# Dense layer with squared ReLU: the first block's loads, transposes and tail columns arranged anew, w2 in three loads

## The chip, the cores and the metric

The kernel runs on one core of one Trainium2 chip. A core has five engines that run beside each other and meet at semaphores: TensorE (PE in the profile, with PEld for its weight loads), VectorE (DVE), ScalarE (ACT), GpSimd (POOL) and SyncE (SP), which here only issues transfers. Transfers run on 16 DMA engines. The metric is device time in microseconds (us), lower is better: the median over several executions.

## The reference

```python
# x (1, 2048, 576), w1 (576, 4608), b1 (4608), w2 (4608, 576), b2 (576), all bf16
h = jnp.einsum("bsd,df->bsf", x, w1) + b1
r = jnp.where(h > 0, h, 0)
h = r * r
out = jnp.einsum("bsf,fd->bsd", h, w2) + b2
```

Both products have 2048 x 576 x 4608 multiplications. The inner dimension of the first, 576, is four and a half times the 128 rows of TensorE's array.

## The kernel before

The 2048 rows of x are worked in four blocks of 512 (`SB`). For each block the kernel needs x transposed (`xTw`, 576 rows as nine slots of 64 on two halves of the partitions), computes the hidden values as 36 tiles of 128 columns of w1 (`hT`), and then multiplies by w2. Blocks 0 and 1 go first, hidden values of both and then the second product of both; blocks 2 and 3 follow in the same way.

Of the 36 hidden tiles, four (`G`) use full matmuls on `w1n`: 512 rows of w1 in four parts of 128 (index k), and the 64 rows left over in `w1n8`, used by two half-height matmuls side by side (`pair`, lines 203 and 205). The other 32 tiles are in `w1_h`: 16 columns j for the lower half of the partitions and 16 for the upper, and `a_rows` (line 179) runs for each j nine pairs of 64-row matmuls, lower and upper at once (lines 188 and 190). For this, most of x transposed has to stand on both halves of the partitions; `dup_windows` (lines 119 and 120) copies it over with VectorE. Each hidden tile is then read out by ScalarE (relu with the bias, line 176) and squared by VectorE (line 177).

Block 0 has its own start, since nothing is loaded yet; blocks 1 to 3 get x transposed by the DMA engines (`load_xT`). For block 0 the four x tiles of 128 rows are loaded as they are (`load_x`, line 72) and TensorE transposes them (`x_transpose`, line 149: four full 128-column parts each and, for the 64 tail columns, a fifth transpose of the last 128 columns), while ScalarE and VectorE copy the results out of PSUM (`x_copies`, lines 156 to 159). The first hidden tiles of block 0 are computed with k outermost and in two halves of 256 rows (`part(h, k)`, line 227: half h of the block, part k, four matmuls). The order on TensorE is written out by hand: seven warming matmuls on constants (line 63), transposes of tiles 0 and 1, part(0,0), transposes of tile 2, parts (0,1) and (0,2), transposes of tile 3, parts (0,3) and (1,0), the transpose of b1 (`make_b1T`, line 166), the remaining parts, the pairs, and then `a_rows(0)`.

All transfers keep their order in the program on the queue that issues them. SP's queue issues x tile 0, w1n parts 0 and 1, x tile 3, w1n parts 2 and 3; then w1_h columns j=0 for each half, w1n8 in two loads (line 79), w1_h to j=11, the transposed x of block 1, w1_h to j=15, b2 (line 304), w2 in six loads (line 134), and the transposed x of block 2. ScalarE's queue issues x tiles 1 and 2 ahead of its table load; GpSimd's issues b1's rows and a column of b2. An SP issue of w1_h is 144 or 288 KB, in runs of 256 or 512 bytes.

PSUM has eight banks, four in the pool `ps_h` and four in `ps_o`; a tile waits until an earlier one of its pool is read out.

Of the kernel before, what the change touches and what calls it, by code (L numbers as in the profile page):

```python
# [11 lines left out]
BF16 = mybir.dt.bfloat16  # L12
FP32 = mybir.dt.float32
# [4 lines left out]
def kernel(  # L18
# [9 lines left out]
    nc = tc.nc  # L28
    keep = tc.keep_in_program_order
    P = 128  # L30
    H = 64
    x2 = x.flatten_outer_dims()
    out2 = out.flatten_outer_dims()
    S, D = x2.shape
    F = w1.shape[1]
    NFT = F // P
    NC = D // H
    NK = NC // 2
    G = 4
    GW = G * P  # L40
# [4 lines left out]
    RT = SB // P  # L45
    DT = P
    DM = D - DT

    const = ctx.enter_context(tc.tile_pool(name="const", bufs=1))
    wpool = ctx.enter_context(tc.tile_pool(name="wpool", bufs=1))  # L50
# [5 lines left out]
    ps_h = ctx.enter_context(tc.tile_pool(name="ps_h", bufs=4, space=PSUM))  # L56
    ps_o = ctx.enter_context(tc.tile_pool(name="ps_o", bufs=4, space=PSUM))

    wps = ps_o.tile([P, 512], FP32, name="wps", tag="po")
    ones = nc.const_aps.tensor(1.0, [P, 512], BF16)  # L60
    WARM = [512] * 6 + [128]
    for i, n in enumerate(WARM):
        keep(nc.tensor.matmul(wps[:, 0:n], lhsT=ones[:, 0:P], rhs=ones[:, 0:n], start=True, stop=True))  # L63

    xs = const.tile([P, RT, D], BF16, name="x_sb")
    w1n = wpool.tile([P, NK, GW], BF16, name="w1n")
    w1n8 = wpool.tile([P, G // 2, P], BF16, name="w1n8")
    w1_h = wpool.tile([P, NC, FH], BF16, name="w1_h")
    w1_v = w1.rearrange("(c p) f -> p c f", p=H)

    def load_x(eng, rt):
        keep(eng.dma_start(out=xs[:, rt, :], in_=x2[rt * P:(rt + 1) * P, :]))

    def load_w1n(eng, k):
        keep(eng.dma_start(out=w1n[:, k, :], in_=w1[k * P:(k + 1) * P, 0:GW]))

    def load_w1n8(eng, h):
        src = w1[NK * P:D, 0:GW].rearrange("p (i h f) -> p i h f", h=2, f=P)
        keep(eng.dma_start(out=w1n8[h * H:(h + 1) * H, :, :], in_=src[:, :, h, :]))

    def load_w1(eng, h, j0, j1):
        keep(eng.dma_start(out=w1_h[h * H:(h + 1) * H, :, j0 * P:j1 * P],
                      in_=w1_v[:, :, GW + h * FH + j0 * P:GW + h * FH + j1 * P]))

    load_x(nc.sync, 0)
    load_x(nc.scalar, 1)
    load_w1n(nc.sync, 0)
    load_x(nc.scalar, 2)
    load_w1n(nc.sync, 1)
    load_x(nc.sync, 3)  # L90
    for k in range(2, NK):
        load_w1n(nc.sync, k)

    ident = const.tile([P, P], BF16, name="ident")
    make_identity(nc, ident[:])
    b1_rows = const.tile([P, P], BF16, name="b1_rows")
    nc.gpsimd.memset(b1_rows[:], 0.0)
    nc.gpsimd.dma_start(out=b1_rows[0:NFT, :], in_=b1.rearrange("(ft p) -> ft p", p=P))
    b2_col = const.tile([P, 1], BF16, name="b2_col")
    nc.gpsimd.dma_start(out=b2_col[:], in_=b2[DM:D].rearrange("(d o) -> d o", o=1))  # L100
    b2T = const.tile([P, 1], FP32, name="b2T")
    nc.gpsimd.tensor_copy(out=b2T[:], in_=b2_col[:])
    warm = const.tile([P, 1], FP32, name="warm")
    keep(nc.scalar.activation(out=warm[:], in_=nc.const_aps.tensor(0.0, [P, 1], FP32), func=ACT.Relu))

    E3, O, SPC, E = 0, 1, 5, 6
    LO_W = [O, O + 1, O + 2, O + 3, E, E + 1, E + 2, E3, SPC]
# [9 lines left out]
    def dup_windows(sb):  # L117
        xT = xT_blk[sb]
        keep(nc.vector.tensor_copy(out=xT[0:H, SPC:SPC + 4, :], in_=xT[H:P, E3:E3 + 4, :]))  # L119
        keep(nc.vector.tensor_copy(out=xT[H:P, SPC:SPC + 4, :], in_=xT[0:H, O:O + 4, :]))  # L120
# [7 lines left out]

    w2_sb = wpool.tile([P, NFT, D], BF16, name="w2_sb")
    w2_view = w2.rearrange("(ft p) d -> p ft d", p=P)  # L130
    W2CH = 6

    def load_w2(c):
        keep(nc.sync.dma_start(out=w2_sb[:, c * W2CH:(c + 1) * W2CH, :], in_=w2_view[:, c * W2CH:(c + 1) * W2CH, :]))
# [3 lines left out]
    alloc_xT(0)  # L138
    xT0 = xT_blk[0]
    HS = SB // 2  # L140
    tb_po = [ps_o.tile([P, 2, HS], BF16, name="tb", tag="po") for _ in range(2)]
    tb_ph = [ps_h.tile([P, 2, HS], BF16, name="tb", tag="ph") for _ in range(4)]
    half_banks = [tb_ph, None]

    def x_transpose(j, k):
        h, q = divmod(j, 2)
        qc = slice(q * P, (q + 1) * P)
        bank, slot, c0 = (half_banks[h][k], 0, k * P) if k < NK else (half_banks[h][2], 1, D - P)
        keep(nc.tensor.transpose(bank[:, slot, qc], xs[:, j, c0:c0 + P], ident[:]))  # L149

    def x_copies(h):
        hc = slice(h * HS, (h + 1) * HS)
        for k in range(NK):
            src = half_banks[h][k][:, 0, :]
            if k % 2 == 0:
                keep(nc.vector.tensor_copy(out=xT0[:, O + k, hc], in_=src))  # L156
            else:
                keep(nc.scalar.copy(out=xT0[:, O + k, hc], in_=src))
        keep(nc.vector.tensor_copy(out=xT0[:, E3, hc], in_=half_banks[h][2][:, 1, :]))


    b1T = const.tile([P, NFT], FP32, name="b1T")

    def make_b1T():
        b1T_ps = ps_o.tile([P, P], BF16, name="b1T_ps", tag="po")
        keep(nc.tensor.transpose(b1T_ps[:], b1_rows[:], ident[:]))  # L166
        keep(nc.vector.tensor_copy(out=b1T[:], in_=b1T_ps[:, 0:NFT]))

# [26 lines left out]
    def a_full(sb, order):  # L195
        xT = xT_blk[sb]
        banks = []
        for g in range(G):
            pool, tag = (ps_o, "po") if g < 2 else (ps_h, "ph")
            banks.append(pool.tile([P, SB], FP32, name="pn", tag=tag))  # L200

        def pair(i, start, stop):
            keep(nc.tensor.matmul(banks[2 * i][:], lhsT=w1n8[0:H, i, :], rhs=xT[0:H, SPC, :],  # L203
                             start=start, stop=stop, skip_group_check=order == "k_outer"))
            keep(nc.tensor.matmul(banks[2 * i + 1][:], lhsT=w1n8[H:P, i, :], rhs=xT[H:P, E3, :],  # L205
                             start=start, stop=stop, skip_group_check=order == "k_outer"))

        def full(g, k, start, stop):
            keep(nc.tensor.matmul(banks[g][:], lhsT=w1n[:, k, g * P:(g + 1) * P], rhs=xT[:, O + k, :],  # L209
                             start=start, stop=stop))  # L210

        if order == "rows_first":
            for i in (1, 0):
                pair(i, True, False)
            for g in (2, 3, 0, 1):
                for k in range(NK):
                    full(g, k, False, k == NK - 1)
                evac_h(sb, banks[g], g)
        else:
            if order == "k_outer":  # L220
                tb_new = [ps_h.tile([P, 2, HS], BF16, name="tb", tag="ph") for _ in range(2)]
                half_banks[1] = tb_new + tb_po

                def part(h, k):
                    hc = slice(h * HS, (h + 1) * HS)
                    for g in range(G):
                        keep(nc.tensor.matmul(banks[g][:, hc], lhsT=w1n[:, k, g * P:(g + 1) * P],  # L227
                                              rhs=xT[:, O + k, hc], start=(h == 0 and k == 0), stop=False,
                                              skip_group_check=True))

                for j in range(2):
                    for k in range(NK):
                        x_transpose(j, k)
                for j in range(2):
                    x_transpose(j, NK)
                x_copies(0)
                part(0, 0)
                for k in range(NK + 1):
                    x_transpose(2, k)
                part(0, 1)  # L240
                part(0, 2)
                for k in range(NK + 1):
                    x_transpose(3, k)
                x_copies(1)
                dup_windows(0)
                part(0, 3)
                part(1, 0)
                make_b1T()
                for k in range(1, NK):
                    part(1, k)  # L250
            else:
                for g in (2, 3, 0, 1):
                    for k in range(NK):
                        full(g, k, k == 0, False)
            for i in (1, 0):
                pair(i, False, True)
                evac_h(sb, banks[2 * i], 2 * i)
                evac_h(sb, banks[2 * i + 1], 2 * i + 1)
# [35 lines left out]
    for (j0, j1) in [(0, 1), (1, 2), (2, 4), (4, 6), (6, 8), (8, 10), (10, 12)]:  # L294
        load_w1(nc.sync, 0, j0, j1)
        load_w1(nc.sync, 1, j0, j1)
        if j0 == 0:
            load_w1n8(nc.sync, 0)
            load_w1n8(nc.sync, 1)
    load_xT(1)  # L300
    for (j0, j1) in [(12, 14), (14, 16)]:
        load_w1(nc.sync, 0, j0, j1)
        load_w1(nc.sync, 1, j0, j1)
    keep(nc.sync.dma_start(out=b2_bc[:], in_=b2.partition_broadcast(P)))
    for c in (0, 3, 1, 4, 2, 5):
        load_w2(c)
    load_xT(2)

# [51 lines left out]
```

## Time and profile before

| | |
|---|---|
| median of 7 executions | 291.11 us (290.91 to 291.48) |
| the profiled execution's own time | 291.04 us |
| its span, first to last instruction | 289.2 us |
| TensorE busy | 285.3 us, 2032 matmuls |
| TensorE weight loads busy | 159.0 us |
| ScalarE busy | 96.7 us |
| VectorE busy | 78.5 us |
| GpSimd busy | 2.3 us |
| DMA | 31637 packets, 16.52 MB |

Busy times are of one execution. A matmul's busy time overlaps that of the next, so TensorE's busy share says that it has work, not that it runs at its peak. In a line of groups, "xN" is the count, then come busy us, mean ns of one, and the engine's idle time just ahead of those instructions, with what ended most of it. In the chain of waits each line is a start, a length and what ran. "DMA to landing" is the time from a transfer's issue to the signal that all of it has arrived.

### The profile page before, as it was taken

To read this page: it belongs to the slowest core of one execution; us is meant where nothing else is said; L and a number is where in the kernel's file an instruction comes from. 1 tells how busy PE (TensorE), PEld (TensorE's weight loads), DVE (VectorE), ACT (ScalarE), POOL (GpSimd) and SP (SyncE) were. 2 spreads that over 40 slices of the span, in tenths; PEclk is the share of its full clock that TensorE was granted. 3 is DMA by queue.
4 is the path that set the end of the run, shared out by engine and by line. 5 is a ranking of instruction groups with operands and counts; after the bars stand their busy time and mean duration, and the time that the engine had idled before them with its cause. 6 is when DMAs were issued, how large, how long until landed. Compare 5 with 4: busy or idle time off the path is not lost.

```text
span 289.2 us, 4699 instructions
## 1 busy us (share of the span) xinstructions
PE 285.3 (99%) x2032; PEld 159.0 (55%) x2032; DVE 78.5 (27%) x176; ACT 96.7 (33%) x154; POOL 2.3 (1%) x10
## 2 busy tenths in 40 slices
PE   8999999999999999999999999999999999999995
PEld 5568888887444555555544444444444455555554
DVE  1644544444500200000025444444440001000001
ACT  3666666666400000000027666666670000000000
POOL 3000000000000000000000000000000000000000
PEclk9999999999999999999999999999999999999999
DMA  6999999700001100000000000000000110000000
GB/s 195 220 240 179 275 387 255 104 0 2 0 18 37 35 16 18 16 16 18 16 16 2 1 2 0 2 0 2 0 2 0 36 39 16 16 17 32 19 16 18
DMA packets 31637, 16.52 MB, mean 57 GB/s; under 512 B 15732, under 2 KB 31616, under 8 KB 31616
## 3 DMA queue, kind: packets, MB, share of 16 engines
q1 hardware_dynamic: 31264, 15.91, 22.6%
q8 instruction: 16, 0.26, 0.4%
q10 hardware_dynamic: 288, 0.30, 0.3%
q14 instruction: 5, 0.04, 0.0%
q0 software_dynamic: 64, 0.01, 0.0%
HBM read 11.36 MB, written 2.36 MB: 47 GB/s over the span
## 4 chain that ended last, share of the span: by engine, by line
PE 99%; DVE 0%; issue 0%
PE po L289 38%; PE ph L188 35%; PE pt L270 11%; PE ph L190 8%; PE pn L209 4%; PE pn L227 1%; PE wps L63 1%; PE pn L203 1%; PE tb L149 0%; DVE xTw L156 0%; DVE o_sb L291 0%; PE pn L205 0%; PE b1T_ps L166 0%
## 5 line engine op out<-in xcount | busy, mean ns | idle before, releaser
L190 PE MATMUL ph<-xTw,w_h 64*128 64x512 bf16 x576 | 124.7, 376 | 0.0
L188 PE MATMUL ph<-xTw,w_h 64*128 64x512 bf16 x576 | 124.6, 376 | 0.0
L289 PE MATMUL po<-w_sb,hT 128*128 128x448 bf16 (+2 forms) x612 | 109.4, 341 | 0.0
L176 ACT ACTIVATE r<-ph,b1T 128x512 bf16<-128x512 f32 x128 | 81.1, 685 | 41.6 <-PE ph L190 22.7
L289 PEld LDWEIGHTS <-hT 128*128 128x128 bf16 x612 | 58.5, 98 | 51.0
L177 DVE TENSOR_TENSOR hT<-r 128x512 bf16<-128x512 bf16 x144 | 61.2, 425 | 76.0 <-ACT r L176 75.8
L188 PEld LDWEIGHTS <-w_h 64*128 64x128 bf16 x576 | 54.1, 94 | 48.3
L190 PEld LDWEIGHTS <-w_h 64*128 64x128 bf16 x576 | 54.1, 94 | 0.2 <-DMA w_h<-in_w_dram 0.2
L291 DVE TENSOR_TENSOR o_sb<-po,b_bc 128x448 bf16<-128x448 f32 (+2 forms) x17 | 10.1, 597 | 125.8 <-PE po L289 125.8
L270 PE MATMUL pt<-hT,w_sb 128*128 128x512 bf16 x144 | 31.4, 379 | 0.0
L176 ACT ACTIVATE r<-pn,b1T 128x512 bf16<-128x512 f32 x16 | 10.3, 688 | 61.1 <-PE pn L205 59.6
L270 PEld LDWEIGHTS <-w_sb 128*128 128x128 bf16 x144 | 14.1, 98 | 17.0
L273 ACT ACTIVATE oT<-pt,b2T 128x512 bf16<-128x512 f32 x4 | 2.8, 688 | 28.3 <-PE pt L270 28.3
L209 PE MATMUL pn<-xTw,w1n 128*128 128x512 bf16 x48 | 10.9, 379 | 0.0
L209 PEld LDWEIGHTS <-w1n 128*128 128x128 bf16 x48 | 4.5, 97 | 6.0 <-issue 0.8
L227 PE MATMUL pn<-xTw,w1n 128*128 128x256 bf16 x32 | 4.2, 273 | 0.1
L63 PE MATMUL wps<-const-bfloat16-1.0 128*128 128x512 bf16 (+1 forms) x7 | 2.8, 581 | 0.8 <-PEq L344 0.8
L227 PEld LDWEIGHTS <-w1n 128*128 128x128 bf16 x32 | 2.9, 97 | 0.8 <-DMA w1n<-in_w_dram 0.3
L119 DVE COPY xTw<-xTw 64x2048 bf16<-64x2048 bf16 x4 | 2.8, 689 | 0.2
L120 DVE COPY xTw<-xTw 64x2048 bf16<-64x2048 bf16 x4 | 2.8, 688 | 0.1
L156 DVE COPY xTw<-tb 128x256 bf16<-128x256 bf16 x4 | 1.1, 292 | 5.9 <-PE tb L149 5.9
L203 PE MATMUL pn<-xTw,w1n 64*128 64x512 bf16 x8 | 2.4, 379 | 0.0
(23 smaller groups left out, 14.3 us busy)
## 6 DMA issues: line engine op xcount, KB each, us to landing
w_sb<-in_w_dram SPq DMA_DIRECT2D x6, 864.0 KB, 11.2
w_h<-in_w_dram SPq DMA_DIRECT2D x14, 288.0 KB, 5.7
out_dram<-o_sb SPq DMA_DIRECT2D x15, 112.0 KB, 1.7
w_h<-in_w_dram SPq DMA_DIRECT2D x4, 144.0 KB, 3.5
w1n<-in_w_dram SPq DMA_DIRECT2D x4, 128.0 KB, 3.3
out_dram<-ot SPq DMA_DIRECT2D x4, 128.0 KB, 2.0
x_sb<-in_x_dram ACTq DMA_DIRECT2D x2, 144.0 KB, 3.1
x_sb<-in_x_dram SPq DMA_DIRECT2D x2, 144.0 KB, 3.1
```

The source lines that it names most:

```text
L63: keep(nc.tensor.matmul(wps[:, 0:n], lhsT=ones[:, 0:P], rhs=ones[:, 0:n], start=True, stop=True))
L119: keep(nc.vector.tensor_copy(out=xT[0:H, SPC:SPC + 4, :], in_=xT[H:P, E3:E3 + 4, :]))
L176: keep(nc.scalar.activation(out=r[:], in_=bank[:], func=ACT.Relu, bias=b1T[:, ft:ft + 1], scale=1.0))
L177: keep(nc.vector.tensor_tensor(out=hTs[sb][:, ft, :], in0=r[:], in1=r[:], op=ALU.mult))
L188: keep(nc.tensor.matmul(bx[:], lhsT=w1_h[0:H, LO_C[i], jc], rhs=xT[0:H, LO_W[i], :], start=(i == 0), stop=(i == NC - 1)))
L190: keep(nc.tensor.matmul(by[:], lhsT=w1_h[H:P, UP_C[i], jc], rhs=xT[H:P, UP_W[i], :], start=(i == 0), stop=(i == NC - 1)))
L203: keep(nc.tensor.matmul(banks[2 * i][:], lhsT=w1n8[0:H, i, :], rhs=xT[0:H, SPC, :], start=start, stop=stop, skip_group_check=order == "k_o ...
L209: keep(nc.tensor.matmul(banks[g][:], lhsT=w1n[:, k, g * P:(g + 1) * P], rhs=xT[:, O + k, :], start=start, stop=stop))
L227: keep(nc.tensor.matmul(banks[g][:, hc], lhsT=w1n[:, k, g * P:(g + 1) * P], rhs=xT[:, O + k, hc], start=(h == 0 and k == 0), stop=False, s ...
L270: keep(nc.tensor.matmul(pt[:], lhsT=w2_sb[:, ft, DM:D], rhs=hT[:, ft, :], start=(i == 0), stop=(i == NFT - 1)))
L289: keep(nc.tensor.matmul(po[:, 0:d1 - d0], lhsT=hT[:, ft, jj * P:(jj + 1) * P], rhs=w2_sb[:, ft, d0:d1], start=(i == 0), stop=(i == NFT - 1)))
L291: keep(nc.vector.tensor_tensor(out=o_sb[:, d0:d1], in0=po[:, 0:d1 - d0], in1=b2_bc[:, d0:d1], op=ALU.add))
```

## The change

The diff changes block 0's start and two loads further on:

- Loads. x tile 0 comes in two pieces of columns, 0 to 255 on SP's queue and 256 to 575 on ScalarE's. All four x tiles are issued ahead of w1n (tiles 1 and 3 on SP, tile 2 on ScalarE). w1n comes in three loads, k=0 and k=2,3 on ScalarE's queue, k=1 on SP's. w1n8 comes in one load on SP's queue ahead of all of w1_h; it now holds all 512 columns on both halves of the partitions, and its source reads the 64 rows of w1 twice. b1's rows are loaded from ScalarE's queue after its table load, b2's column from SP's after w1_h.
- Transposes. All four x tiles are transposed, four parts each, ahead of the first part(0,0). Copies out of PSUM are VectorE's, but for the last two, ScalarE's. The tail columns of two x tiles are first put side by side by GpSimd (`xs8`), so that one transpose does both; four VectorE copies put them into place.
- Duplicates. `dup_windows(0)` is replaced by one ScalarE copy of three slots (`dup_windows_first`), one VectorE copy of four and one of one.
- One warming matmul fewer; PSUM tiles of the start move from `ps_o` to `ps_h`, and block 0's four first banks are all in `ps_o`.
- w2 comes in three loads of twelve row tiles.

The diff, cut to its core:

```diff
...
     ps_h = ctx.enter_context(tc.tile_pool(name="ps_h", bufs=4, space=PSUM))
     ps_o = ctx.enter_context(tc.tile_pool(name="ps_o", bufs=4, space=PSUM))
-    wps = ps_o.tile([P, 512], FP32, name="wps", tag="po")
+    wps = ps_h.tile([P, 512], FP32, name="wps", tag="ph")
     ones = nc.const_aps.tensor(1.0, [P, 512], BF16)
-    WARM = [512] * 6 + [128]
+    WARM = [512] * 5 + [128]
     for i, n in enumerate(WARM):
         keep(nc.tensor.matmul(wps[:, 0:n], lhsT=ones[:, 0:P], rhs=ones[:, 0:n], start=True, stop=True))
     xs = const.tile([P, RT, D], BF16, name="x_sb")
     w1n = wpool.tile([P, NK, GW], BF16, name="w1n")
-    w1n8 = wpool.tile([P, G // 2, P], BF16, name="w1n8")
+    w1n8 = wpool.tile([P, GW], BF16, name="w1n8")
     w1_h = wpool.tile([P, NC, FH], BF16, name="w1_h")
     w1_v = w1.rearrange("(c p) f -> p c f", p=H)
-    def load_x(eng, rt):
-        keep(eng.dma_start(out=xs[:, rt, :], in_=x2[rt * P:(rt + 1) * P, :]))
-
-    def load_w1n(eng, k):
-        keep(eng.dma_start(out=w1n[:, k, :], in_=w1[k * P:(k + 1) * P, 0:GW]))
-
-    def load_w1n8(eng, h):
-        src = w1[NK * P:D, 0:GW].rearrange("p (i h f) -> p i h f", h=2, f=P)
-        keep(eng.dma_start(out=w1n8[h * H:(h + 1) * H, :, :], in_=src[:, :, h, :]))
+    def load_x(eng, rt, c0=0, c1=D):
+        keep(eng.dma_start(out=xs[:, rt, c0:c1], in_=x2[rt * P:(rt + 1) * P, c0:c1]))
+
+    def load_w1n(eng, k0, k1):
+        src = w1[k0 * P:k1 * P, 0:GW].rearrange("(k p) f -> p k f", p=P)
+        keep(eng.dma_start(out=w1n[:, k0:k1, :], in_=src))
+
+    def load_w1n8(eng):
+        src = w1[NK * P:D, 0:GW].unsqueeze(0).broadcast_to([2, H, GW])
+        keep(eng.dma_start(out=w1n8[:, :], in_=src))
     def load_w1(eng, h, j0, j1):
         keep(eng.dma_start(out=w1_h[h * H:(h + 1) * H, :, j0 * P:j1 * P],
                       in_=w1_v[:, :, GW + h * FH + j0 * P:GW + h * FH + j1 * P]))
-    load_x(nc.sync, 0)
-    load_x(nc.scalar, 1)
-    load_w1n(nc.sync, 0)
+    b1_rows = const.tile([P, P], BF16, name="b1_rows")
+    nc.vector.memset(b1_rows[:], 0.0)
+    load_x(nc.sync, 0, 0, 2 * P)
+    load_x(nc.scalar, 0, 2 * P, D)
+    load_x(nc.sync, 1)
     load_x(nc.scalar, 2)
-    load_w1n(nc.sync, 1)
     load_x(nc.sync, 3)
-    for k in range(2, NK):
-        load_w1n(nc.sync, k)
+    load_w1n(nc.scalar, 0, 1)
+    load_w1n(nc.sync, 1, 2)
+    load_w1n(nc.scalar, 2, NK)
     ident = const.tile([P, P], BF16, name="ident")
     make_identity(nc, ident[:])
-    b1_rows = const.tile([P, P], BF16, name="b1_rows")
-    nc.gpsimd.memset(b1_rows[:], 0.0)
-    nc.gpsimd.dma_start(out=b1_rows[0:NFT, :], in_=b1.rearrange("(ft p) -> ft p", p=P))
-    b2_col = const.tile([P, 1], BF16, name="b2_col")
-    nc.gpsimd.dma_start(out=b2_col[:], in_=b2[DM:D].rearrange("(d o) -> d o", o=1))
-    b2T = const.tile([P, 1], FP32, name="b2T")
-    nc.gpsimd.tensor_copy(out=b2T[:], in_=b2_col[:])
     warm = const.tile([P, 1], FP32, name="warm")
     keep(nc.scalar.activation(out=warm[:], in_=nc.const_aps.tensor(0.0, [P, 1], FP32), func=ACT.Relu))
+    load_w1n8(nc.sync)
+    keep(nc.scalar.dma_start(out=b1_rows[0:NFT, :], in_=b1.rearrange("(ft p) -> ft p", p=P)))
+    xs8 = const.tile([P, RT, H], BF16, name="xs8")
+    for h in range(2):
+        keep(nc.gpsimd.tensor_copy(out=xs8[:, 2 * h:2 * h + 2, :], in_=xs[:, 2 * h:2 * h + 2, NK * P:D]))
     E3, O, SPC, E = 0, 1, 5, 6
     LO_W = [O, O + 1, O + 2, O + 3, E, E + 1, E + 2, E3, SPC]
...
     w2_sb = wpool.tile([P, NFT, D], BF16, name="w2_sb")
     w2_view = w2.rearrange("(ft p) d -> p ft d", p=P)
-    W2CH = 6
+    W2CH = 12
     def load_w2(c):
         keep(nc.sync.dma_start(out=w2_sb[:, c * W2CH:(c + 1) * W2CH, :], in_=w2_view[:, c * W2CH:(c + 1) * W2CH, :]))
...
     alloc_xT(0)
     xT0 = xT_blk[0]
     HS = SB // 2
-    tb_po = [ps_o.tile([P, 2, HS], BF16, name="tb", tag="po") for _ in range(2)]
-    tb_ph = [ps_h.tile([P, 2, HS], BF16, name="tb", tag="ph") for _ in range(4)]
-    half_banks = [tb_ph, None]
-
-    def x_transpose(j, k):
+    tb = [[ps_h.tile([P, 4, HS], BF16, name="tb", tag="ph") for _ in range(2)] for _ in range(2)]
+
+    def x_transpose(j):
         h, q = divmod(j, 2)
-        qc = slice(q * P, (q + 1) * P)
-        bank, slot, c0 = (half_banks[h][k], 0, k * P) if k < NK else (half_banks[h][2], 1, D - P)
-        keep(nc.tensor.transpose(bank[:, slot, qc], xs[:, j, c0:c0 + P], ident[:]))
-
-    def x_copies(h):
         hc = slice(h * HS, (h + 1) * HS)
-        for k in range(NK):
-            src = half_banks[h][k][:, 0, :]
-            if k % 2 == 0:
-                keep(nc.vector.tensor_copy(out=xT0[:, O + k, hc], in_=src))
-            else:
-                keep(nc.scalar.copy(out=xT0[:, O + k, hc], in_=src))
-        keep(nc.vector.tensor_copy(out=xT0[:, E3, hc], in_=half_banks[h][2][:, 1, :]))
-
+        for bank in range(2):
+            for k in range(2 * bank, 2 * bank + 2):
+                keep(nc.tensor.transpose(tb[h][bank][:, k % 2, q * P:(q + 1) * P], xs[:, j, k * P:(k + 1) * P], ident[:]))
+            for k in range(2 * bank, 2 * bank + 2) if q == 1 else ():
+                copy = nc.scalar.copy if h == 1 and bank == 1 else nc.vector.tensor_copy
+                keep(copy(out=xT0[:, O + k, hc], in_=tb[h][bank][:, k % 2, :]))
     b1T = const.tile([P, NFT], FP32, name="b1T")
+    def dup_windows_first():
+        keep(nc.scalar.copy(out=xT0[0:H, E:E + 3, :], in_=xT0[H:P, O:O + 3, :]))
+
+    def transpose_tails():
+        tl = ps_h.tile([P, 2, P], BF16, name="tl", tag="ph")
+        for h in range(2):
+            keep(nc.tensor.transpose(tl[:, h, :], xs8[:, 2 * h:2 * h + 2, :], ident[:]))
+        x8 = xT0.rearrange("p c (h q t) -> p c h q t", h=2, q=2)
+        for q in range(2):
+            keep(nc.vector.tensor_copy(out=x8[H:P, E3, :, q, :], in_=tl[q * H:(q + 1) * H, 0:2, :]))
+        for q in range(2):
+            keep(nc.vector.tensor_copy(out=x8[0:H, SPC, :, q, :], in_=tl[q * H:(q + 1) * H, 0:2, :]))
+        keep(nc.vector.tensor_copy(out=xT0[H:P, SPC:SPC + 4, :], in_=xT0[0:H, O:O + 4, :]))
+        keep(nc.vector.tensor_copy(out=xT0[0:H, E3, :], in_=xT0[H:P, O + 3, :]))
+
     def make_b1T():
-        b1T_ps = ps_o.tile([P, P], BF16, name="b1T_ps", tag="po")
+        b1T_ps = ps_h.tile([P, P], BF16, name="b1T_ps", tag="ph")
         keep(nc.tensor.transpose(b1T_ps[:], b1_rows[:], ident[:]))
         keep(nc.vector.tensor_copy(out=b1T[:], in_=b1T_ps[:, 0:NFT]))
...
         xT = xT_blk[sb]
         banks = []
         for g in range(G):
-            pool, tag = (ps_o, "po") if g < 2 else (ps_h, "ph")
+            pool, tag = (ps_o, "po") if g < 2 or order == "k_outer" else (ps_h, "ph")
             banks.append(pool.tile([P, SB], FP32, name="pn", tag=tag))
         def pair(i, start, stop):
-            keep(nc.tensor.matmul(banks[2 * i][:], lhsT=w1n8[0:H, i, :], rhs=xT[0:H, SPC, :],
+            keep(nc.tensor.matmul(banks[2 * i][:], lhsT=w1n8[0:H, 2 * i * P:(2 * i + 1) * P], rhs=xT[0:H, SPC, :],
                              start=start, stop=stop, skip_group_check=order == "k_outer"))
-            keep(nc.tensor.matmul(banks[2 * i + 1][:], lhsT=w1n8[H:P, i, :], rhs=xT[H:P, E3, :],
+            keep(nc.tensor.matmul(banks[2 * i + 1][:], lhsT=w1n8[H:P, (2 * i + 1) * P:(2 * i + 2) * P], rhs=xT[H:P, E3, :],
                              start=start, stop=stop, skip_group_check=order == "k_outer"))
         def full(g, k, start, stop):
...
                 evac_h(sb, banks[g], g)
         else:
             if order == "k_outer":
-                tb_new = [ps_h.tile([P, 2, HS], BF16, name="tb", tag="ph") for _ in range(2)]
-                half_banks[1] = tb_new + tb_po
-
                 def part(h, k):
                     hc = slice(h * HS, (h + 1) * HS)
                     for g in range(G):
...
                                               rhs=xT[:, O + k, hc], start=(h == 0 and k == 0), stop=False,
                                               skip_group_check=True))
-                for j in range(2):
-                    for k in range(NK):
-                        x_transpose(j, k)
-                for j in range(2):
-                    x_transpose(j, NK)
-                x_copies(0)
+                for j in range(RT):
+                    x_transpose(j)
+                dup_windows_first()
                 part(0, 0)
-                for k in range(NK + 1):
-                    x_transpose(2, k)
                 part(0, 1)
+                transpose_tails()
                 part(0, 2)
-                for k in range(NK + 1):
-                    x_transpose(3, k)
-                x_copies(1)
-                dup_windows(0)
                 part(0, 3)
-                part(1, 0)
-                make_b1T()
-                for k in range(1, NK):
+                for k in range(NK):
                     part(1, k)
+                    if k == 1:
+                        make_b1T()
             else:
                 for g in (2, 3, 0, 1):
                     for k in range(NK):
...
     for (j0, j1) in [(0, 1), (1, 2), (2, 4), (4, 6), (6, 8), (8, 10), (10, 12)]:
         load_w1(nc.sync, 0, j0, j1)
         load_w1(nc.sync, 1, j0, j1)
-        if j0 == 0:
-            load_w1n8(nc.sync, 0)
-            load_w1n8(nc.sync, 1)
     load_xT(1)
     for (j0, j1) in [(12, 14), (14, 16)]:
         load_w1(nc.sync, 0, j0, j1)
         load_w1(nc.sync, 1, j0, j1)
+    b2_col = const.tile([P, 1], BF16, name="b2_col")
+    keep(nc.sync.dma_start(out=b2_col[:], in_=b2[DM:D].rearrange("(d o) -> d o", o=1)))
+    b2T = const.tile([P, 1], FP32, name="b2T")
+    keep(nc.gpsimd.tensor_copy(out=b2T[:], in_=b2_col[:]))
     keep(nc.sync.dma_start(out=b2_bc[:], in_=b2.partition_broadcast(P)))
-    for c in (0, 3, 1, 4, 2, 5):
+    for c in range(3):
         load_w2(c)
     load_xT(2)
```

## The prediction

> **What bounds the kernel now.** I read the page's first and fourth parts, then the chain of waits over the first 10 us, then the weight loads' idle time, then each early transfer's landing.
>
> ```profile
> PE 285.3 (99%) x2032; PEld 159.0 (55%) x2032; DVE 78.5 (27%) x176; ACT 96.7 (33%) x154; POOL 2.3 (1%) x10
> PE 99%; DVE 0%; issue 0%
> ```
>
> TensorE is busy for 99% of the span and is the whole chain. From 9.3 us on it runs pairs of 64-row matmuls with hardly a hole, and the diff touches none of those matmuls. So only what moves the first w1_h matmul, or opens a hole in the w1_h rows, can move the end. The chain at the start:
>
> ```profile
> 0.78 2.83 PE wps L63 x7
> 3.60 0.67 PE tb L149 x5
> ...
> 4.29 0.30 DVE xTw L156
> ...
> 6.89 0.87 PE pn L227 x8
> 7.76 0.06 PE b1T_ps L166
> 7.82 1.31 PE pn L227 x12
> 9.13 0.32 PE pn L203
> ```
>
> Transposes, halves of the k-outer product and warming matmuls lie against each other without a hole of note. The pair matmuls load weights at 9.06 and the first w1_h weights load at 9.29. Weight loads' holes:
>
> ```profile
> L190 PEld LDWEIGHTS <-w_h 64*128 64x128 bf16 x576 | 54.1, 94 | 0.2 <-DMA w_h<-in_w_dram 0.2
> L227 PEld LDWEIGHTS <-w1n 128*128 128x128 bf16 x32 | 2.9, 97 | 0.8 <-DMA w1n<-in_w_dram 0.3
> ```
>
> ```profile
> 17.34 0.09 PEld L190 LDWEIGHTS <-w_h 64*128 64x128 bf16 x1 [0.19 <-DMA w_h<-in_w_dram]
> ```
>
> The second hole is at 17.34 us, for the second half of w1_h columns j=4,5. That load was issued at 9.84:
>
> ```profile
> L82 SPq DMA_DIRECT2D w_h<-in_w_dram x1: 638/638/638, 9.8 to 9.8; - x1
>   PEld L190: 0.2, 1
> DMA to landing us min/median/max: 7.5/7.5/7.5
> ```
>
> 9.84 + 7.5 = 17.3. So the w1_h stream runs just behind TensorE: the first two loads land at 3.68 + 3.8 = 7.5 and 4.45 + 3.6 = 8.0 (needed 9.29, 1.3 us to spare), those of j=2,3 by 8.48 + 4.5 = 13.0 (needed at about 13.4), those of j=4,5 too late by 0.2. In the landing records each load adds 16 increments to its semaphore; 15 of this one are in by 15.84, the last at 17.30, behind one 16 KB instruction packet of 1.2 us at 14.0.
>
> **What the Trainium skill says.** "DMA: Bandwidth & Descriptors", section "Why a DMA increments its semaphore by 16 and not by 1": a transfer runs on the largest k up to 16 that divides the slowest dimension of both its access patterns. Its "Rules for kernel authors" say that "a leading zero-stride broadcast of c copies" confines the whole transfer to at most c engines. In the trace before, all transfers whose slowest dimension is 64 or 128 spread their 16 increments over time, which agrees; no broadcast with a small leading dimension occurs, so the price of one isn't shown. "TensorE: Matmul & The Clock Gate", Part 1: full clock comes after about 3.4 us of sustained work. The trace's clock record turns to full at 4.17 us, 3.39 us after the first matmul at 0.78: agrees.
>
> **The change, part by part.**
>
> *w1n8, where I put the cost.* Before: two loads of 32 KB, 256-byte packets, on 16 engines. After: one load of 128 rows of 1,024 bytes whose source is a broadcast with a leading dimension of 2. By the rule k = 2: 64 rows on each of two DMA engines. The trace's packet records give 46 ns for a 1,024-byte packet, 51 for 1,152, 18 for 256 and 27 to 28 for 512 when the engines aren't all pressed (35 to 40 when they are).
>
> What such an engine has to move up to there: x, 8 x 27 (first piece) + 8 x about 32 (second, between the neighbours) + 3 x 8 x 51 = 1.70 us; w1n, 32 x 46 = 1.47; w1n8, 64 x 46 = 2.94. Sum 6.11 us. Before, 85 KB had moved by 2.5 us and then 190 KB per 0.5 us, which is like a start at full rate at 2.28. End: 8.4; with the 0.5 us from last data to landing (x tiles 0 and 1 are moved by about 3.05, landed by 3.55), 8.9. TensorE's pairs need it at about 9.3: just in time.
>
> But w1_h queues behind it on those two engines, and each w1_h load has rows for all 16. Columns j=0: 2 x 36 packets x 18 ns = 1.30 us, landing 8.9 + 1.3 = 10.2 where 9.29 was the time before. Everything on TensorE from there starts 0.95 later. Columns j=1: another 1.3, 11.5, needed at 10.25 + 1.94 = 12.2 (nine pairs at 0.2155 us). j=2,3: 72 x 28 to 36 ns = 2.0 to 2.6, 13.5 to 14.1, needed at 14.1. j=4,5: 15.5 to 16.7, with an instruction packet 1.2 more, needed at 18.0. So the 0.2 wait at 17.34 is gone. Net +0.95 - 0.2 = **+0.75 us**. Bounds: 16 engines after all, 8 x 46 = 0.37 us, no cost; or the two engines some 0.7 us slower all along (before, the slowest engine's increment came that much after the first) and j=2,3 late too, +1.7.
>
> *Issue order.* The trace shows eight completion semaphores taken in turn by both hardware queues; issue n waits for landing n-8 (the first w1_h load at 3.68 waits for x tile 1, landed 3.66). After, eight transfers precede w1n8: it is issued when the first x piece lands, about 3.3, and w1_h from about 4.0 in steps of 0.67, the j=4 loads some 1.1 us earlier than before (two w1n8 issues of 0.65 are gone). One of those shares w1n8's semaphore and waits for its landing at 8.9; the two slow engines have 2.6 + 2 us of queued rows by then, so this costs nothing. If w1n8 lands early, these earlier issues are the gain that removes the wait at 17.34.
>
> *All of x first.* Nothing of the product starts before tile 3. x tile 3 moves from 2.13 to 1.66 on SP's queue; 720 KB precede or share its way against 851 KB, so it lands at about 5.1 instead of 5.6. Then 4 transposes, 0.25, part(0,0) from 5.45 (before 4.64), 32 halves at 0.109 = 3.5, two tail transposes and b1's 0.2, w1n waits of 0.1 (k=1 and the joint k=2,3 load land by about 6.0 and 6.5): pairs at 9.25 to 9.3 against 9.06, +0.2. This lies inside the 0.95 above; alone it would cost 0.2. One warming matmul less (0.43) and two transposes less are swallowed by waiting for x.
>
> *Copies and tails.* VectorE: six copies of 0.29, the last at about 6.1; four tail copies, about 0.28 each by L159's row (0.279), from 6.6 to 7.7; the 64x2048 copy 0.69, a 64x512 about 0.2, b1T 0.2: 8.9. Cover: pairs at 9.3 need the tails (7.7), the evacuation behind them b1T. Uncovered it would cost up to 0.5. GpSimd's xs8 copies, 0.2 each after tile 3: 5.6, needed at 6.35. ScalarE: table load moves behind four issues to 2.7 to 4.0, needed at 5.4; the 64x1536 duplicate is not in the trace: by "ScalarE: Activation LUTs", "What ACT_TABLE_LOAD costs", 186 ns + 0.833 per element, an estimated 1.5 us, 2.0 by the slope between the rows of 374 and 688 ns, so done by 8.2; window E is wanted at 10.2. Behind it on ScalarE are evacuations that can't start before 9.5. b1's rows go to ScalarE's queue at about 4.2, land by 7.8, wanted at 8.3.
>
> *w2 in three loads of twelve, b2's column on SP.* w2 is first read at about 76 us and landed before by about 49: 27 us of cover. b2T is first wanted at 83.8. Nothing.
>
> **Sum.** Profiled span 289.2 + 0.75 = 289.95; the profiled run took 291.04, 1.84 outside the span; its median of runs is 291.11, 0.07 above. So 289.95 + 1.84 + 0.07 = 291.86, put at **291.9**. A measurement of this kernel can tell about 0.2%, 0.58 us, from no change.
>
> **Rivals.**
> - *The load spreads over 16 engines.* For it: every load in the trace does. Against: the skill's rule names this very shape. Pairs +0.2, wait of 0.2 gone: 291.1. The wait moves to the x tiles.
> - *The start gets faster, the other side.* The stream of w1_h sets the end at 17.34, and its issues come 1.1 us earlier. If x tile 3 lands by 4.6 and w1n8 on 16 engines, pairs start at 8.75 and no wait follows: 0.3 + 0.2 gained, 290.6. It decides only if tile 3 lands 0.5 us before my 5.1; 720 KB at the measured rate speak against.
> - *The clock stays low.* TensorE now works some 2.24 of the first 3.4 us densely and then waits between tiles. If the full clock comes a window later, at 7.6, the halves run at 0.213 until then: 2.15 us do 10 instead of 20, 1.1 lost, transposes 0.2, pairs at 10.55, first w1_h weights at 10.75: +1.45 - 0.2, 292.4. Against: x's transposes fill much of the gap.
>
> **How the numbers follow.** Two-engine load with a full clock 0.60, between 291.4 and 292.8; 16 engines 0.18 (290.8 to 291.5); faster start 0.05; low clock or further late loads 0.17 (292.0 to 293.5). Range 290.9 to 293.2: it leaves out most of the third and the far end of the fourth. Slower by over 0.2%: 0.7 of 0.60, nearly all of the fourth and a little of the second, with the two-engine bounds reaching further up than down, 0.66. Within: 0.27. Faster: 0.07.
>
> **What would show it.** Right: two of w1n8's 16 increments late, its landing 5 to 6 us after issue; a hole on PEld ahead of the first L190/L188 weights, released by w_h's DMA, of some 0.7 us, and none at j=4. Wrong: w1n8 in 3 us and no such hole; or the hole ahead of the pairs, released by VectorE (tails) or by the x tiles; or 256-column halves 0.213 us apart after 5.4 us (clock). A hole later than 20 us would mean that I missed a wait altogether.

## The result

| | before | changed |
|---|---|---|
| median | 291.15 us (290.76 to 291.80, 34 executions) | 292.63 us (291.88 to 294.16, 14 executions) |
| profiled execution, its span | 291.04, 289.2 us | 292.05, 290.1 us |

The ratio is 1.0058 (95% interval 1.0047 to 1.0069): 0.6% or 1.5 us slower in the median. The fastest execution is only 1.1 slower, and the changed kernel's times lie over 2.3 us where the other's lie over 1.0; one more execution is on record, of 295.01, which isn't among the 14. This looks like a part that every execution pays and one that only some do. The profiled one is among the fastest, so I read the first part from it. Page of the changed kernel, busy times and the chain by engine:

```profile
PE 285.1 (98%) x2029; PEld 139.1 (48%) x2029; DVE 79.2 (27%) x181; ACT 97.6 (34%) x153; POOL 1.7 (1%) x9
...
PE 96%; DMA 3%; SPq 0%; DVE 0%; issue 0%
```

Three matmuls fewer and the same busy time, but TensorE is no longer the whole chain: transfers hold 3% of it. The chain of waits at the start (start, length, what):

```profile
1.18 2.90 DMA x_sb<-in_x_dram
4.08 0.05 issue
4.13 0.21 PE tb L149
4.34 5.02 DMA b_rows<-in_b_dram
9.36 0.04 issue
9.41 0.23 PE b1T_ps L173
9.64 0.87 PE pn L231 x8
10.51 0.32 PE pn L210
```

Five of the first ten us hang on one transfer of 9 KB, b1's rows, which in the prediction had half a microsecond to spare. The weight loads of the changed kernel in order of time (start, length, what; in brackets the idle time ahead and what ended it):

```profile
2.97 0.36 PEld L149 LDWEIGHTS <-x_sb 128*128 128x128 bf16 x4 [0.39 <-DMA x_sb<-in_x_dram]
4.12 1.22 PEld L149 LDWEIGHTS <-x_sb 128*128 128x128 bf16 x12 [0.79 <-DMA x_sb<-in_x_dram]
...
9.40 0.10 PEld L173 LDWEIGHTS <-b_rows 128*128 128x128 bf16 x1 [1.40 <-DMA b_rows<-in_b_dram]
...
10.67 0.09 PEld L195 LDWEIGHTS <-w_h 64*128 64x128 bf16 x1
```

The first w1_h weights load at 10.67 against 9.29 in the kernel before:

```profile
9.29 0.09 PEld L188 LDWEIGHTS <-w_h 64*128 64x128 bf16 x1
```

No hole follows; the one at 17.34 is gone:

```profile
L197 PEld LDWEIGHTS <-w_h 64*128 64x128 bf16 x576 | 54.1, 94 | 0.0
```

The last matmul ends 1.30 us later (287.47 against 286.17); the rest of the span happened to be 0.36 shorter.

The landing records say why b1 is late. A transfer on 16 DMA engines leaves 16 marks, one for each engine; on fewer engines one early mark stands for those that aren't used. These are the marks of four transfers (us):

```
w1n8, one broadcast load, issued 3.11:   4.19 (one mark, for 14 of 16)  9.52  9.55
b1's rows, issued 4.34:                  5.15 (one mark, for 4)  6.22 ... 7.14 (10 engines)  9.33  9.36
w1_h j=0, lower, issued 3.86:            6.60 ... 7.38 (14 engines)  10.03  10.09
w1_h j=0, upper, issued 4.57:            7.48 ... 7.97 (14 engines)  10.48  10.53
```

w1n8 ran on two engines, as the Trainium skill has it ("DMA: Bandwidth & Descriptors", section "Why a DMA increments its semaphore by 16 and not by 1"): the increments for 14 engines came at once, the last two when the data had landed, 6.4 us after the issue. The three transfers below it in the table, issued while it ran and from either queue, came late on just two engines each. b1 held TensorE first; had it not, w1_h would have done so 0.14 us earlier at most (10.53 against 10.67).

### The profile page after: what moved, and what is told of

Same layout as the page of the kernel before. It is cut to its first block, busy times and chain, and to the rows that moved or that the text cites. A ratio compares the mean times of both kernels' runs of the same rounds, so it can differ in the third digit from the quotient of the medians.

```text
span 290.1 us, 4700 instructions
## 1 busy us (share of the span) xinstructions
PE 285.1 (98%) x2029; PEld 139.1 (48%) x2029; DVE 79.2 (27%) x181; ACT 97.6 (34%) x153; POOL 1.7 (1%) x9
## 4 chain that ended last, share of the span: by engine, by line
PE 96%; DMA 3%; SPq 0%; DVE 0%; issue 0%
PE ph L195 42%; PE po L285 38%; PE pt L266 11%; PE pn L216 4%; DMA b_rows<-in_b_dram 2%; DMA x_sb<-in_x_dram 1%; PE ph L197 1%; PE pn L210 1%; PE pn L231 0%; SPq L72 0%; DVE o_sb L287 0%; PE b1T_ps L173 0%; PE tb L149 0%; PE pn L212 0%
## 5 line engine op out<-in xcount | busy, mean ns | idle before, releaser
L149 PE MATMUL tb<-ident,x_sb 128*128 128x128 bf16 x16 | 2.1, 307 | 0.5 <-DMA x_sb<-in_x_dram 0.5
L210 PE MATMUL pn<-xTw,w1n 64*128 64x512 bf16 x8 | 2.4, 379 | 0.0
L212 PE MATMUL pn<-xTw,w1n 64*128 64x512 bf16 x8 | 2.4, 379 | 0.0
```

The costliest lines, as they stand in the source:

```text
L210: keep(nc.tensor.matmul(banks[2 * i][:], lhsT=w1n8[0:H, 2 * i * P:(2 * i + 1) * P], rhs=xT[0:H, SPC, :], start=start, stop=stop, skip_grou ...
```

## The experiments

Ratios are to runs of the kernel before on the same chip. Three chips were used (medians of the kernel before: 291.39, 291.35 and 291.21).

**w1n8 on 16 engines.** The changed kernel with

```diff
-        src = w1[NK * P:D, 0:GW].unsqueeze(0).broadcast_to([2, H, GW])
-        keep(eng.dma_start(out=w1n8[:, :], in_=src))
+        for h in range(2):
+            keep(eng.dma_start(out=w1n8[h * H:(h + 1) * H, :], in_=w1[NK * P:D, 0:GW]))
```

> The changed kernel with its small w1 rows (w1n8) in two loads of 64 rows, one for each half of the partitions, in place of the one broadcast load. Theory (the broadcast load runs on two DMA engines, and what queues behind it there, b1's rows and the first w1_h columns, comes late): both loads spread over 16 engines and land by about 7; b1's rows land by 7.3 although they are still issued at 4.3; no hole of more than 0.1 us ahead of the b1 transpose nor ahead of the first w1_h weights; those load at 9.4 to 9.6 instead of 10.67; 1.1 to 1.3 us less than the changed kernel, about 291.2 to 291.5. Rival A (b1's rows are late because they are issued behind ScalarE's table load): the 1.4 us hole at the b1 transpose stays, and so does the time. Rival B (the clock, full at 5.4 instead of 4.2 us, costs the time): the time stays within 0.3 us of the changed kernel's and stays as spread out.

Measured: 1.0042 (1.0022 to 1.0062), median 292.82, 290.89 to 294.80. The loads landed at 6.65 and 6.88, b1 at 6.70 and the first w1_h at 7.47, and no weight load waited for b1 or w1_h. Rival A is out: b1 is issued behind the table load here as well. But the time hardly fell: the interval overlaps the changed kernel's. The chain of this run:

```profile
1.67 3.46 DMA x_sb<-in_x_dram
5.13 0.05 issue
5.18 0.61 PE tb L149 x4
5.79 1.71 PE pn L231 x8
7.49 0.21 PE tl L162 x2
7.71 2.45 PE pn L231 x16
10.16 0.06 PE b1T_ps L173
10.22 0.87 PE pn L231 x8
```

The first eight halves take 1.71 us and the last eight 0.87: TensorE ran at half clock until 9.02, by the trace's clock record (before: 4.17; the changed kernel's profiled execution: 5.37). The first w1_h matmul started at 11.46, where the changed kernel's started at 10.89, and from 5.13 on no transfer stands in the chain. The fastest of the 20 executions, 290.89, is level with the fastest of the kernel before (290.85); the slowest is almost 4 us behind it. So rival B, the late clock, which I had held apart from the cause, looks like a second cause.

**b1 early.** The changed kernel with b1's rows issued from GpSimd at the start.

```diff
     make_identity(nc, ident[:])
+    nc.gpsimd.dma_start(out=b1_rows[0:NFT, :], in_=b1.rearrange("(ft p) -> ft p", p=P))
...
-    keep(nc.scalar.dma_start(out=b1_rows[0:NFT, :], in_=b1.rearrange("(ft p) -> ft p", p=P)))
```

> The changed kernel with b1's rows issued from GpSimd's queue at about 1.3 us, as in the kernel before, and all else as changed. Theory (two slow engines): b1's rows land by 5.5 and the hole ahead of its transpose goes, but TensorE then waits for the second w1_h load, which still lands at about 10.5: first w1_h weights at 10.5 to 10.6 instead of 10.67, a hole of about 1.1 us there, and a time within 0.3 us of the changed kernel's. Rival A (b1's late issue is the cause): first w1_h weights at 9.5, 1.2 us less.

Measured: 1.0055 (1.0043 to 1.0066), nothing gained. The wait moved where the two engines put it next, to w1_h (weight loads of this run; two more waits for w1_h follow, 0.22 at 14.59 and 0.37 at 18.62):

```profile
10.39 0.09 PEld L195 LDWEIGHTS <-w_h 64*128 64x128 bf16 x1 [0.33 <-DMA w_h<-in_w_dram]
...
10.80 0.09 PEld L197 LDWEIGHTS <-w_h 64*128 64x128 bf16 x1 [0.32 <-DMA w_h<-in_w_dram]
```

**The broadcast load alone.** The kernel before with w1n8 in one broadcast load ahead of w1_h, its tile and the pairs' slices as in the change.

```diff
     for k in range(2, NK):
         load_w1n(nc.sync, k)
+    load_w1n8(nc.sync)
...
-        if j0 == 0:
-            load_w1n8(nc.sync, 0)
-            load_w1n8(nc.sync, 1)
```

> The kernel before with one part of the change alone: w1n8 in one broadcast load, ahead of w1_h. Theory (two slow engines): issued at 3.7, landed at 9.2 to 9.8, the first w1_h loads at 10.0 to 10.7; TensorE waits for w1n8 at the pairs (up to 0.7) or for w1_h (in all about 1.0 to 1.4 at the first w1_h weights), nothing at the b1 transpose, since b1 was issued ahead of w1n8; 0.8 to 1.3 us slower than the kernel before, 292.0 to 292.5. Rival A (b1's late issue) and rival B (x tiles first, clock): no more than 0.2 us slower than before.

Measured: 1.0024 (1.0016 to 1.0032), 0.7 us slower, a little under what was expected. w1n8 landed at 9.41, the two w1_h loads at 9.92 and 10.38; the clock was full only at 6.71 in this execution, so TensorE came to w1_h late by itself and waited there for 0.33 (and 0.17 once more, at 14.16):

```profile
10.42 0.09 PEld L191 LDWEIGHTS <-w_h 64*128 64x128 bf16 x1 [0.33 <-DMA w_h<-in_w_dram]
```

In this execution the late clock and the late load overlap: TensorE waits only for the time by which the load is later than its own work.

**Eight warming matmuls.** The changed kernel with

```diff
-    WARM = [512] * 5 + [128]
+    WARM = [512] * 8 + [128]
```

> The changed kernel with eight warming matmuls of 512 columns instead of five, so that TensorE is dense until 4.3 us. Theory (two slow engines): the clock is full by about 4.2, but the b1 transpose still waits until about 9.4 and the first w1_h weights load at 10.6 to 10.7; the fastest executions are as fast as the changed kernel's, 291.9 to 292.1. If a clock that stays or falls low makes the slow ones among its executions (293 to 294), these go and the median falls by 0.3 to 0.6. Rival B (the clock is the main cost): 1 us or more less, also in the fastest.

Measured: 1.0021 (1.0010 to 1.0033), median 291.93; all but one of 20 lie from 291.32 to 292.63. Against the changed kernel's 1.0058 this took away 0.37%, 1.1 us where I had expected 0.3 to 0.6, and the fastest gained 0.6 too. That is near what rival B had (1 us or more, also in the fastest). The two-engine load is still there; b1's transpose waits less, since TensorE arrives later:

```profile
9.32 0.10 PEld L173 LDWEIGHTS <-b_rows 128*128 128x128 bf16 x1 [0.73 <-DMA b_rows<-in_b_dram]
```

**Both edits.** w1n8 in two loads and eight warming matmuls.

> The changed kernel with both edits of the first two lookers: w1n8 in two loads of 64 rows, and eight warming matmuls. Theory (the change costs time in two places, the load on two DMA engines and a clock that turns full late because TensorE waits between x tiles): with both gone the median is within 0.3 us of the kernel before (290.9 to 291.5) and the spread is as narrow as the kernel before has it, about 1.2 us; first w1_h weights load at 9.6 to 9.9. If either edit alone did the work, the median stays near that of the warming edit alone (291.9). Rival C (putting all of x first costs by itself): 0.3 us or more above the kernel before.

Measured: 1.0007 (1.0000 to 1.0014), 290.97 to 291.97. The chain of this run is TensorE from the first microsecond, at full clock when the halves begin:

```profile
0.77 3.68 PE wps L63 x9
4.45 1.27 PE tb L149 x16
5.72 0.87 PE pn L231 x8
6.59 0.11 PE tl L162 x2
6.70 1.75 PE pn L231 x16
```

The table that decides (ratio to the kernel before):

| warming matmuls of 512 | broadcast w1n8 | two loads |
|---|---|---|
| five | 1.0058 (the change) | 1.0042 |
| six | not run | 1.0008 |
| eight | 1.0021 | 1.0007 |

Down the first column three more warming matmuls are worth 0.37%, 1.1 us; along the last row the two engines are worth 0.14%, 0.4 us (the intervals overlap a little). The other way round it is nearly the same: 0.16% along the first row, where the intervals overlap widely, then 0.35% down the second column. So in these ratios the two parts add up, and no overlap of the kind seen in one execution above shows. 0.07%, 0.2 us, stays for all else, putting x first among it. The interval allows up to 0.4 us, so rival C (0.3 or more) is unlikely, not excluded.

**Which edit makes the clock late.** Two loads with six warming matmuls (the diff as above with 6 for 8), and the kernel before with five.

> The changed kernel with w1n8 in two loads and one warming matmul of 512 columns given back (six, as in the kernel before). Which part of the change makes the clock late? If it is the warming matmul taken away: the time comes down from 1.0042 to about 1.0007 of the kernel before, as with eight. If it is the waits between the x tiles (0.4 to 0.6 us, twice): one more matmul fills only the first of them; the time stays at 1.002 to 1.004, with executions at 293 and above.

Measured: 1.0008 (0.9998 to 1.0018); one execution of 20 at 293.37, two at 292.1, the others up to 291.7.

> The kernel before with one warming matmul of 512 columns fewer, that edit alone. If the matmul taken away makes the clock late: 1.002 or more of the kernel before. If it is the waits between the x tiles: x tile 0 lands at 3.5, 0.4 us of gap, within 0.1% of the kernel before.

Measured: 0.9998 (0.9989 to 1.0006). So the answer is neither of the two that I had put up: the matmul taken away costs nothing in the old order, and given back it mends the new one (with w1n8 in two loads). It takes both, the missing matmul and the new order of work. That the waits between the x tiles are what matters in the new order is my reading; no run changes them alone.

**The warming matmuls alone.** The kernel before without its six warming matmuls of 512 columns.

```diff
-    WARM = [512] * 6 + [128]
+    WARM = [128]
```

> The kernel before with its six warming matmuls of 512 columns taken away (the one of 128 stays), all loads and the order of work as before. No work is delayed by this, since x tile 0 lands at 3.5 anyway. Theory (the late clock is a cost of its own): the clock turns full at 6 to 10.5 us instead of 4.2 to 7, the first w1_h weights load 0.5 to 2.5 us later, the median rises by 1 to 2 us and the executions spread over 2 us or more. If the clock doesn't matter at the start: within 0.2 us of the kernel before.

Measured: 1.0031 (1.0019 to 1.0044), 291.55 to 293.38. All transfers and all useful work were as before. The chain of this run:

```profile
0.73 2.57 DMA x_sb<-in_x_dram
3.31 0.05 issue
3.35 1.25 PE tb L149 x10
4.60 0.86 PE pn L227 x4
5.46 0.53 PE tb L149 x5
5.99 1.27 PE pn L227 x8
```

The first four halves take 0.86 us, where they took 0.60 in the profile before; the clock was full at 6.67. But this execution, 291.67, is one of the faster ones, and the clock was as late in two profiles of the old order with all the warming matmuls: at 6.71 with the broadcast load alone and at 6.62 with w2 in three loads. So the times show that work that computes nothing is worth 0.3% here; that the clock is what takes it isn't shown, since no execution of 292 us or more was profiled here.

**The other part, and tries for a faster kernel.** The kernel before with w2 in three loads; with w1n8's two loads from GpSimd's queue; with both; and with w1n part 2 moved to ScalarE's queue besides.

```diff
-    W2CH = 6
+    W2CH = 12
...
-    for c in (0, 3, 1, 4, 2, 5):
+    for c in range(3):
```

> The kernel before with w2 in three loads of twelve row tiles, in order, instead of six. Every theory: w2 lands some 27 us before it is read, so within 0.2 us of the kernel before.

Measured: 0.9991 (0.9983 to 1.0000).

```diff
+    load_w1n8(nc.gpsimd, 0)
+    load_w1n8(nc.gpsimd, 1)
...
-            load_w1n8(nc.sync, 0)
-            load_w1n8(nc.sync, 1)
```

> The kernel before with its two w1n8 loads issued from GpSimd's queue at about 2.1 us instead of from SP's between the first w1_h loads. Theory: SP issues w1_h from the third load on some 1.3 us earlier, so the wait of 0.2 us at j=4 goes, and executions whose clock turns early gain too; 0.1 to 0.4 us less than the kernel before. If the w1_h stream isn't a bound there: no difference, or slower by the 0.1 to 0.3 us that x tile 3 and w1n come later behind the 64 KB.

Measured: 0.9989 (0.9982 to 0.9996), 0.3 us faster; no weight load waited for w1_h in its profile. With both edits:

> The kernel before with w1n8 from GpSimd's queue and w2 in three loads, the two edits that were 0.9989 and 0.9991 of the kernel before, together. If both gains are real and apart: 0.998. If the one of w2 was chance (its cover is 27 us): 0.999.

Measured: 0.9996 (0.9988 to 1.0005). And with w1n part 2 moved:

```diff
     load_x(nc.scalar, 2)
+    load_w1n(nc.scalar, 2)
```

> As the run before, and w1n part 2 issued from ScalarE's queue at 1.6 us instead of from SP's at 2.6, part 3 on SP at 2.6. With a clock that turns early, TensorE waited 0.5 us for part 2 (landed 5.87); this lands it by 5.3. Expected 0.0 to 0.3 us less than the run before; if the clock turns late in most executions, nothing.

Measured: 1.0000 (0.9991 to 1.0009). The small gains didn't add up: where the two edits stood together, on another chip, the interval includes no change. One of the four, w1n8 from GpSimd's queue, beat the kernel before by more than its interval, and by 0.1% only; whether that would hold elsewhere is open.

## Why the prediction was right or wrong

*Slower, and within the range: right.* 292.63 lies in 290.9 to 293.2. The point, 291.9, was half of the way: +0.75 forecast, +1.5 measured. That the range held is in part luck: of the two parts of the loss, the sum had one and put the other, the larger, at nothing.

*w1n8 on two engines: right.* Two marks late, 6.4 us from issue to landing instead of the 5 to 6 that I gave: 9.55 instead of 8.9. The last of its packets moved at 9.02, where the sum of packet times had 8.4. The first w1_h weights loaded at 10.67 instead of 10.25, in this execution, which is +1.38 where the term was +0.95. By the ratios the two engines are worth less: 0.4 us in the new order, 0.7 with the broadcast load alone in the old one. So the net +0.75 was about the size of this part.

*Where it would show: wrong.* I looked for a hole ahead of the first w1_h weights; it was ahead of the b1 transpose. The step that failed is "b1's rows go to ScalarE's queue at about 4.2, land by 7.8": I took a small transfer on the other queue to pass the two busy engines in turn. On ten engines it was there by 7.14, on those two at 9.36. That had no price of its own, since w1_h was as late (the run with b1 early).

*The wait at 17.34 gone: right, but not for the reason given.* The two j=4,5 loads landed at 15.54 and 16.75, as forecast (15.5 to 16.7), and TensorE came 1.4 us later. But they were not issued 1.1 us earlier. "w1_h from about 4.0 in steps of 0.67" failed: two of SP's issues took 1.72 us each, so these loads went out at 10.34 and 11.02 instead of the 9.16 and 9.84 before. (The instruction packet of the trace before starts at 14.44, not at 14.0; nothing in the sum changes by it.)

*"One warming matmul less (0.43) and two transposes less are swallowed by waiting for x": this is the step that failed, and the larger part of the miss.* The time was swallowed, but the matmul also kept TensorE dense. Without it, and with waits of 0.4 to 0.8 us ahead of the x tiles, the clock turned full late: at 9.02 in the profile of the first experiment, where the halves ran at up to twice their time, and, as I infer from the spread of the times, in many other executions. Three more warming matmuls took away 1.1 us. The rival named this, at 0.17 and 292.4; the median is nearer to it than to my likeliest case. "Against: x's transposes fill much of the gap" was no good argument, since it didn't say how dense is dense enough. Between the fastest executions the broadcast load makes 1.0 us with five warming matmuls (291.88 against 290.89), but only 0.35 with eight (291.32 against 290.97), so the fastest don't show the two engines alone. Taking away the two engines left 1.0042, taking away the late clock 1.0021, and only both together ended the loss (1.0007).

*x first, copies and tails, w2 and b2: right.* With both edits the pairs' weights loaded at 9.31 against 9.06 before, so the x order made them no more than 0.25 later; VectorE's tails ended at 8.8 and held nothing; ScalarE's duplicate took 1.47 us, by the Trainium skill ("ScalarE: Activation LUTs", section "What ACT_TABLE_LOAD costs") 186 + 0.833 x 1536 ns = 1.47, and was hidden. w2 moved nothing that could be told from chance.

*What stays open.* The timed executions have a mean clock each, but no record of when it turned, so that those above 293 us lose their time to the clock is an inference. In all 13 profiles that have a clock record, the first stretch of full clock lasted 283.31 or 286.72 us, which are 83 and 84 times 3.413 us. So the clock seems to be set once in each step of 3.413 us, and where these steps fall against the kernel's start differs from execution to execution. In 12 profiles the turn lies between 3.41 and 6.71, within one such step; the turn at 9.02 lies in the next. That would explain both why the turn moves by chance and why a start that isn't dense enough costs a whole step more. How dense is enough isn't shown: TensorE was busy for 2.88 of the 3.41 us ahead of the turn at 5.37, and for 2.92 of the step from 2.20 to 5.61 in the first experiment, after which the clock stayed low.

In six executions, two each of the changed kernel and of the first two experiments, the mean granted clock was 0.994. That fits one more such step at half clock (half of 3.413 us is 0.6% of 290), and they took 293.3 to 294.5. Why the clock was low there isn't shown; the wait for b1 is no likely reason, since the profiles of the two experiments have none. Other executions as slow (294.03, 294.80) have 1.000 and 0.999.

## What to carry to other kernels

A load that reads the same rows twice saves an issue and can pay for it in DMA engines, two instead of 16 here. Look at how many engines' marks a landing has before trusting its size, and expect transfers issued meanwhile to be late on the same engines, whatever their queue. Warming matmuls ahead of the first data are part of the schedule: judge them with the waits that follow. An edit that "costs nothing because TensorE waits anyway" may cost a late clock, as the matmul taken away did here in the new order and not in the old. Where two causes end at the same point, undo each alone and both together before saying what each is worth.

## What the runs showed of the hardware

- A small transfer on ScalarE's queue did not pass a long one of SP's queue on the engines that they shared. Of b1's 36 packets, 30 moved at 5.75 to 6.70 us (ten engines) and the other six at 8.76 to 8.90 (two engines), in turn with w1n8's last ones, up to 9.02. The records don't name the engines; the times fit w1n8's two. With w1n8 on 16 engines all had landed by 6.70.
- The issuing queue felt it too: SP's w1_h issues took 0.67 and 0.63 us, and the third and fourth 1.72 and 1.71; with two loads for w1n8 these two took 0.64 each.
- The time of the full clock moved from one profiled execution to the next by more than the work ahead of it explains: 3.41 to 9.02 us over all these kernels, and 3.42 to 6.62 over those of the old order with six warming matmuls and no broadcast load. With six or more warming matmuls, or in the old order with five, the times of a kernel lay within 0.8 to 1.4 us of its fastest, but for two executions; with five in the new order they lay up to 3.9 us above it.
